# A recurrent attention block and a SiLU block on one core: the state products in quarters of TensorE's columns

## The chip, the core and the metric

The kernel runs on one core of one Trainium2 chip. The metric is the device time of one execution in microseconds, launch to end; the median of repeated runs counts. The kernel before takes 577.69 us (three runs, 577.37 to 578.81).

## What is computed

Two blocks, one behind the other. The first is a gated linear recurrence for 4 batches and 8 heads with 768 tokens and 48 dimensions a head; its output, laid side by side over the heads, feeds a two-layer block with SiLU.

```python
# q, k, v, alpha: (4, 8, 768, 48); alpha between 0.8 and 1.0
for t in range(S):
    state = alpha[:, :, t, :, None] * state + np.einsum('bhd,bhe->bhde', k[:, :, t], v[:, :, t])
    y[:, :, t] = np.einsum('bhd,bhde->bhe', q[:, :, t], state)

x = y.transpose(0, 2, 1, 3).reshape(3072, 384)
h = x @ w_in            # (384, 2048)
g = h * (1.0 / (1.0 + np.exp(-h)))
out = g @ w_out         # (2048, 384)
```

All of it is in fp32.

## The kernel before

The recurrence is cut into chunks of 128 tokens. With 4 batches and 6 chunks in each, 24 chunks are worked through, numbered `n`; `ci` is the place in the sequence, `b` the batch. Two heads make a pair, and a pair lies on 128 partitions: the first head's 48 dimensions on partitions 0 to 47, the second's on 64 to 111, the rest is padding. `NP` is 4 pairs, `D` is 48, `C` is 128.

For a chunk, `products` and `quotient` prepare scaled forms of k and q (`kp`, `qp`); `scores` multiplies them under a causal mask into `g`, and turns `kp` into `kn`, which has the tokens on the partitions; `values` forms y; `states` adds the chunk's contribution to the running state `st`. The state of the last chunk of a batch is not needed, so 20 of the 24 chunks have state products.

`scores`, cut: the products have 48 rows of contraction at partition 0 or 64, and full-width outputs.

```python
        for j in range(NP):
            for u in range(2):
                r = slice(64 * u, 64 * u + D)
                pe.matmul(ps[u][:, j, :], lhsT=c["kp"][r, j, :], rhs=c["qp"][r, j, :],
                          start=True, stop=True)              # L715
        ...
        if ci < NCH - 1:
            ps_k = ps_attn()
            for j in range(NP):
                pe.transpose(ps_k[:, j, :], c["kp"][:, j, :], ident)    # L723
            c["kn"] = work.tile([128, NP, C], F32, name="kn")
            act.copy(c["kn"], ps_k)                           # L725
```

`values` writes y turned, and in quarters: every product has 32 output rows, at partition 0, 32, 64 or 96 of PSUM, so at a quarter of the array's 128 columns. Consecutive products go to different quarters.

```python
        py = ps_attn()
        todo = [(3 * j + i, vn[:, j, at : at + 32], g[:, u, j, :])
                for j in range(NP) for i, at, u in ((0, 0, 0), (1, 32, 0), (2, 80, 1))]
        todo += [(3 * j + 1, vn[:, j, 48:80], g[:, 1, j, :]) for j in range(NP)]
        if ci > 0:
            todo += [(3 * j + i, s[:, j, 32 * i : 32 * i + 32], qp[:, j, :])
                     for j in range(NP) for i in range(3)]
        for i, (at, w, x) in enumerate(todo):
            t, at = divmod(at, 4)
            pe.matmul(py[32 * at : 32 * at + 32, t, :], lhsT=w, rhs=x, ...)   # L749
        ...
        act.copy(xts[half][:, :, e * C : (e + 1) * C], py[:, 0:NKT])          # L754
```

`states` comes next. Its products have 48 output rows, at partition 0 or 64.

```python
            ps = ps_attn()
            for j in range(NP):
                for u in range(2):
                    r = slice(64 * u, 64 * u + D)
                    pe.matmul(ps[r, j, 0:D], lhsT=c["kn"][:, j, r], rhs=vn[:, 2 * j + u, 0:D],
                              start=True, stop=True)          # L764
            for u in range(2):
                r = slice(64 * u, 64 * u + D)
                s, x = st[b][r, :, u, :], ps[r, :, 0:D]
                if ci > 0:
                    dve.tensor_tensor(s, x, s, ALU.add)       # L770
                else:
                    act.copy(s, x)                            # L772
```

`ps_attn()` hands out one of three PSUM buffers in turn; scores, the turned `kp`, y and the states share them.

The two layers of the second block are the large products. They are cut into pieces and put between the stages of the chunks: L807 is the first layer in plain form, L830 the first layer by a scheme with fewer products and more sums, L955 and L928 the second layer in the same two forms. In a step of the main loop the stages stand like this, and `fill` puts pieces behind each slot:

```python
    for step in range(STEPS):
        stages = [[(scores, 1)], [(products, 0)], [(values, 1)], [(states, 1)]]
        if step < GB:                  # GB = 4
            stages = stages[1::-1] + stages[2:]
        elif step >= NA:               # NA = 8
            stages = [[(scores, 1)], [(products, 0)], [(values, 1), (states, 1)], [(quotient, 0)]]
        for slot, group in enumerate(stages):
            for stage, lag in group:
                n = step - lag
                if not 0 <= n < NT:
                    continue
                stage(n)
                ...
            fill(step, slot)
```

The program is not written out strictly in this order: a scheduler places instructions, and may put a later one ahead where an earlier one would have to wait.

The kernel also holds a general path, which runs only when the range of the inputs rules out the quotients; it is not taken here.

Of the kernel before, what the change touches and what calls it, by code (L numbers as in the profile page):

```python
# [355 lines left out]
def quotients(  # L356
# [20 lines left out]
    pe, dve, act, gps = nc.tensor, nc.vector, nc.scalar, nc.gpsimd  # L377
    B, H, S, D = q.shape
# [39 lines left out]
    def ps_attn(n=C):  # L418
        return ps_a.tile([128, 512], F32, name="ps_a").rearrange("p (j c) -> p j c", c=n)
# [335 lines left out]
    def states(n):  # L755
        c = ctxs.pop(n)
        ci, b, vn = c["ci"], c["b"], c["v"]
        if ci < NCH - 1:

            ps = ps_attn()  # L760
            for j in range(NP):
                for u in range(2):
                    r = slice(64 * u, 64 * u + D)
                    pe.matmul(ps[r, j, 0:D], lhsT=c["kn"][:, j, r], rhs=vn[:, 2 * j + u, 0:D],  # L764
                              start=True, stop=True)
            for u in range(2):
                r = slice(64 * u, 64 * u + D)
# [5 lines that stand above are left out]
# [329 lines left out]
    for step in range(STEPS):  # L1102
        stages = [[(scores, 1)], [(products, 0)], [(values, 1)], [(states, 1)]]
        if step < GB:

            stages = stages[1::-1] + stages[2:]
        elif step >= NA:
# [7 lines that stand above are left out]
                if stage is values:  # L1115
                    bridged = n + 1
                if stage is products and n + NIN < NA:
                    load(n + NIN)
                if stage is quotient and n + 1 < NT:
                    load(n + 1)  # L1120
                if stage is states and n + NV < NT:
                    load_v(n + NV)
            fill(step, slot)
            if step >= NA - 1 and slot > 0 and conv_done[1] == NFT and not late:
                settle()
# [20 lines left out]
    ps = ps_attn()[0:1, 0, 0:1]  # L1146
# [64 lines left out]
```

## Time and profile before

| | before |
|---|---|
| median of 3 runs | 577.69 us |
| profiled execution, span | 577.1 us |
| instructions in the profile | 11060 |
| TensorE clock granted | full speed over the whole span |
| DMA | 63.72 MB, 110 GB/s on average |

How to read the profile's views. The page gives each engine's busy time, its share of the span and the number of its instructions; PE is TensorE's matmul, PEld its weight load, which overlaps with matmuls, DVE is VectorE, ACT ScalarE, POOL GpSimd. Below that, the span is cut into 40 equal slices, and each digit is the busy share of a slice in tenths (9 is 90% or more). Matmul ends are modelled, so durations of matmuls that overlap can't be added up; starts and the distances between starts are what to count with.

In the groups of instructions a line has: the line of the kernel, the engine, the operation, output <- inputs, their shapes and types, x count; then busy us and the mean ns of one; then the engine's idle time just before these instructions and what ended it. "issue" is idle time in which the engine waited for nothing that the profile shows. In the view of waits the numbers are the total in us, how many times, and the longest. In the timeline a line has: start in us, duration in us, engine and line, operation, shapes, x how many were merged, and in brackets the idle time before. An fp32 product of this kernel makes two matmul records and two weight loads, a transpose one of each.

### The profile page before, as it was taken

What the parts mean: (1) busy time and instruction counts of PE and PEld (TensorE: products, weight loads), DVE (VectorE), ACT (ScalarE), POOL (GpSimd) and SP (SyncE); (2) the same over time, 40 slices, a digit from 0 to 9 for tenths busy, and PEclk for the clock granted to TensorE, in tenths of its full rate; (3) what the DMA queues carried; (4) which work ended last, traced back from release to release, by engine and by line L of the source; (5) the groups of instructions that cost most, each with busy time, mean ns of one, the idle gap of its engine ahead of it and who ended that gap; (6) DMA issues with size and microseconds to landing.
All of it is one profiled execution on the core that took longest, in us unless ns stands there. A gap on an engine that the chain in (4) does not pass through costs nothing. (4 is left out here: it accounts for less than half of the span.)

```text
span 577.1 us, 11060 instructions
## 1 busy us (share of the span) xinstructions
PE 557.6 (97%) x4450; PEld 491.2 (85%) x4450; DVE 449.3 (78%) x807; ACT 187.6 (33%) x367; POOL 7.3 (1%) x25
## 2 busy tenths in 40 slices
PE   5999999999999999999999999999999999998976
PEld 4677887678998998898998998998998999997976
DVE  5779798999797699995996995996963856747651
ACT  2345543232221233342442442433342331422100
POOL 5000000000000000000000000000000000000000
PEclk9999999999999999999999999999999999999999
DMA  9998784445445414343324333323210123333321
GB/s 212 169 285 215 212 215 118 102 103 139 103 99 129 116 51 120 107 124 84 103 71 118 101 105 85 101 69 89 65 43 9 52 81 115 93 118 98 98 72 30
DMA packets 93900, 63.72 MB, mean 110 GB/s; under 512 B 54800, under 2 KB 85520, under 8 KB 93840
## 3 DMA queue, kind: packets, MB, share of 16 engines
q1 hardware_dynamic: 93840, 62.94, 42.5%
q8 instruction: 36, 0.59, 0.4%
q14 instruction: 24, 0.20, 0.1%
HBM read 58.20 MB, written 4.72 MB: 109 GB/s over the span
## 5 line engine op out<-in xcount | busy, mean ns | idle before, releaser
L928 PE MATMUL ps_o<-w_out,g 128*128 128x192 f32 x704 | 122.8, 328 | 2.3 <-DVE o L942 2.2
L928 PEld LDWEIGHTS ps_o<-w_out,g 128*128 128x128 f32 x704 | 115.2, 190 | 5.6 <-DVE o L942 3.0
L928 PE MATMUL ps_o<-wt,g 128*128 128x192 f32 x528 | 91.6, 326 | 1.3 <-DVE u L1004 1.3
L807 PE MATMUL ps_m<-xt,w_in 128*128 128x256 f32 x384 | 89.6, 384 | 0.8 <-DVE w_in L604 0.5
L928 PEld LDWEIGHTS ps_o<-wt,g 128*128 128x128 f32 x528 | 87.2, 190 | 3.0 <-DVE u L1004 1.6
L807 PEld LDWEIGHTS ps_m<-xt,w_in 128*128 128x128 f32 x384 | 70.7, 190 | 12.2 <-DVE w_in L604 2.9
L830 PE MATMUL ps_m<-xc,w_in 128*128 128x256 f32 x288 | 70.1, 379 | 0.0
L639 DVE TENSOR_REDUCE seen<-bits 128x1 f32<-128x384 int32 (+2 forms) x65 | 42.4, 689 | 30.4 <-DMA bits<-in_moe_w_out_dram 23.9
L830 PEld LDWEIGHTS ps_m<-xc,w_in 128*128 128x128 f32 x288 | 54.0, 190 | 6.4 <-DVE g L844 0.2
L830 PE MATMUL ps_m<-xc,wx 128*128 128x256 f32 x192 | 50.1, 383 | 0.0
L836 ACT COPY g<-ps_m 128x512 f32<-128x512 f32 x64 | 37.0, 586 | 39.8 <-PE ps_m L830 39.8
L933 DVE TENSOR_TENSOR g<-g 128x512 f32<-128x512 f32 x66 | 44.7, 687 | 4.7 <-PE ps_o L928 4.7
L841 ACT ACTIVATE g<-g 128x1024 f32<-128x1024 f32 x32 | 33.2, 1056 | 44.6 <-DVE g L844 44.6
L729 ACT ACTIVATE st<-st,u 128x96 f32<-128x96 f32 x80 | 26.0, 368 | 53.5 <-DVE u L674 38.8
L844 DVE TENSOR_TENSOR g<-ps_m,g 128x512 f32<-128x512 f32 x56 | 37.6, 684 | 2.9 <-PE ps_m L830 2.7
L830 PEld LDWEIGHTS ps_m<-xc,wx 128*128 128x128 f32 x192 | 35.0, 190 | 4.2 <-issue 0.4
L719 DVE TENSOR_TENSOR g<-ps_a,mask 128x512 f32<-128x512 f32 x48 | 31.2, 685 | 6.4 <-PE ps_a L715 6.1
L674 DVE TENSOR_TENSOR_SCAN u<-al,one 128x516 f32<-128x516 f32 x24 | 29.3, 1224 | 6.2 <-ACT al L671 6.1
L699 DVE TENSOR_TENSOR_SCAN p<-al,inv 128x516 f32<-128x516 f32 x24 | 29.5, 1229 | 4.8 <-PE ps_a L749 4.2
L836 ACT COPY part<-ps_m 128x512 f32<-128x512 f32 x32 | 18.8, 587 | 43.6 <-PE ps_m L830 37.8
L810 ACT ACTIVATE g<-ps_m 128x512 f32<-128x512 f32 x32 | 19.0, 594 | 40.6 <-PE ps_m L807 40.5
L715 PEld LDWEIGHTS ps_a<-p,u 48*128 48x128 f32 x384 | 24.8, 193 | 8.1 <-issue 6.5
(117 smaller groups left out, 635.3 us busy)
## 6 DMA issues: line engine op xcount, KB each, us to landing
bits<-in_moe_w_in_dram SPq DMA_DIRECT2D x24, 512.0 KB, 4.2
bits<-in_moe_w_out_dram SPq DMA_DIRECT2D x32, 384.0 KB, 3.4
at<-in_alpha_dram SPq DMA_DIRECT2D x64, 96.0 KB, 2.3
kt<-in_k_dram SPq DMA_DIRECT2D x64, 96.0 KB, 2.4
qt<-in_q_dram SPq DMA_DIRECT2D x64, 96.0 KB, 2.5
vn<-in_v_dram SPq DMA_DIRECT2D x24, 192.0 KB, 3.5
bits<-in_alpha_dram SPq DMA_DIRECT2D x9, 512.0 KB, 3.9
out_dram<-o SPq DMA_DIRECT2D x48, 96.0 KB, 1.8
```

Of the source, the lines that this page charges most:

```text
L639: dve.tensor_reduce(seen[kind][which][:, i : i + 1], x, axis=AX, op=op, apply_absolute_value=True))
L674: dve.tensor_tensor_scan(u[:, end - 1 :: -1], sg[:, end:0:-1], one[:, end:0:-1], 0.0, ALU.mult, ALU.add)
L699: dve.tensor_tensor_scan(p[:, 0:end], sg[:, 0:end], iv[:, 0:end], 0.0, ALU.mult, ALU.add)
L719: dve.tensor_tensor(g[:, u], ps[u], mask[:, None, :].to_broadcast([128, NP, C]), ALU.mult)
L729: act.mul(s[:, j], s[:, j], c["all"][:, j : j + 1])
L807: pe.matmul(ps[:, e, :], lhsT=w_in[:, t, (f + e) * 128 : (f + e + 1) * 128], rhs=xt[:, t, :], start=(t == 0), stop=(t == NKT - 1))
L830: pe.matmul(ps[:, e], lhsT=block_w(w)[:, 2 * pair + e], rhs=block_x(grp, x), start=(first and e == 0), stop=(e == 1), skip_group_check=True)
L836: act.copy(to, ps)
L841: act.activation(x, x, AF.Silu)
L844: dve.tensor_tensor(to, a, b, op)
L928: pe.matmul(ps, lhsT=x, rhs=w[:, i], start=(first and i == 0), stop=(i == HF - 1), skip_group_check=True)
L933: dve.tensor_tensor(cells(grp, h, pair, *to), cells(grp, h, pair, *x), cells(grp, h, pair, *y), ALU.subtract)
```

## The change

The state products are written in quarters of the array's columns: instead of two products of 48 output rows a pair of heads, four of 32. Quarter `i` takes columns 32i to 32i+31 of `kn`, and the v of the head that these belong to. The rows 48 to 63 and 112 to 127 of the PSUM buffer, which come from padding, are written as well now; the instructions that take the result out read the same rows as before. It is for the array to keep the tiling that y, just in front, has used.

```diff
             ps = ps_attn()
             for j in range(NP):
-                for u in range(2):
-                    r = slice(64 * u, 64 * u + D)
-                    pe.matmul(ps[r, j, 0:D], lhsT=c["kn"][:, j, r], rhs=vn[:, 2 * j + u, 0:D],
+                for i in range(4):
+                    r = slice(32 * i, 32 * i + 32)
+                    pe.matmul(ps[r, j, 0:D], lhsT=c["kn"][:, j, r], rhs=vn[:, 2 * j + i // 2, 0:D],
                               start=True, stop=True)
             for u in range(2):
                 r = slice(64 * u, 64 * u + D)
```

## The prediction, made before the changed kernel was run

> **What bounds the kernel now.** I read the head of the page first: busy shares, then the slices over the span.
>
> ```profile
> span 577.1 us, 11060 instructions
> PE 557.6 (97%) x4450; PEld 491.2 (85%) x4450; DVE 449.3 (78%) x807; ACT 187.6 (33%) x367; POOL 7.3 (1%) x25
> ...
> PE   5999999999999999999999999999999999998976
> ...
> DVE  5779798999797699995996995996963856747651
> ```
>
> TensorE is at nine tenths or more from the second slice to the 37th. A busy PE row does not prove that the array streams all the time, so the second view was the waits of PE and of its weight loads between 60 and 470 us: the only wait of the PE row there is one of 0.4 us for VectorE. Only the tail, from 470 us on, has real waits (PE is busy 96.4 of its 107 us), and no state product is left by then: the last starts at 373.4 us. So up to 373 us a nanosecond that PE saves is a nanosecond that everything behind it comes earlier, if nothing takes its place.
>
> The third view, the groups of instructions with shapes kept apart, sizes the line that the change edits (L764) and the one in front of it (L749, y). "x320" counts two records for each fp32 product: 20 chunks of 8 products are 160.
>
> ```profile
> L749 PE MATMUL ps_a<-g,vn 128*32 128x128 f32 x768 | 28.8, 282 | 1.0 <-ACT kn L725 0.7 <-DVE g L719 0.3
> L764 PE MATMUL ps_a<-vn,kn 128*48 128x48 f32 x320 | 11.9, 216 | 0.0
> L764 PEld LDWEIGHTS ps_a<-vn,kn 128*48 128x48 f32 x320 | 9.3, 127 | 4.5 <-issue 4.1 <-DVE w_out L603 0.2 <-ACT st L729 0.2
> ```
>
> All state products together keep PE busy for 11.9 us, 2% of the span. The size of the prize is in the third row: 4.1 us in which the weight load of L764 waited for nothing that the trace can name. The view of all waits of the weight loads tells where such unnamed time sits:
>
> ```profile
> PEld ps_a L749 <- issue: 7.3, 23, 0.5
> PEld ps_a L715 <- issue: 6.5, 22, 0.3
> PEld ps_a L764 <- issue: 4.1, 19, 0.4
> ```
>
> The three longest lines of this view are exactly these three, about once for each run of y (32-wide outputs, all 128 rows), of scores (48 rows) and of states (48-wide outputs). The large products L830 and L928, with six times as many records as L764 (1872 against 320), have at most 0.4 us of it in a group. So it belongs to the change of the array's tiling, not to the products. The fourth view is the timeline of one chunk, weight loads and then products:
>
> ```profile
> 219.39 0.68 PEld L749 LDWEIGHTS ps_a<-p,st 128*32 128x32 f32 x24
> 220.27 0.44 PEld L764 LDWEIGHTS ps_a<-vn,kn 128*48 128x48 f32 x16 [0.20 <-issue]
> 220.76 0.73 PEld L830 LDWEIGHTS ps_m<-xc,wx 128*128 128x128 f32 x4
> ...
> 220.05 0.29 PE L749 MATMUL ps_a<-p,st 128*32 128x128 f32 x4
> ...
> 220.27 0.56 PE L764 MATMUL ps_a<-vn,kn 128*48 128x48 f32 x16
> 220.77 0.48 PE L830 MATMUL ps_m<-xc,wx 128*128 128x256 f32 x1
> ```
>
> **What the Trainium skill says.** "TensorEngine Tiling (Array Packing)", Tiling Modes, Key Properties: changing the tiling mode, not just the tile, drains TensorE. The trace agrees: 0.20 us idle ahead of the first load of states, here and 19 times. The same section: different tiles load and multiply in parallel. The trace agrees for y: 24 loads of 110 ns each take 0.68 us together. "TensorE: Matmul & The Clock Gate", in LDWEIGHTS (loading the stationary operand): the time goes with the columns loaded. In the trace a 32-column load has 110 ns, a 48-column one 125 ns, a 128-column one 190 ns. The same page, Part 1, states a floor of about 25 ns from start to start of small matmuls. States in the trace already start one record per 22 ns on average (below), two tiles side by side, so I take that floor to hold per tile at most.
>
> **The change, part by part.** Each of a chunk's 8 state products, 48 output rows wide at column 0 or 64, becomes two products of 32, at columns 0, 32, 64 and 96, with the same moving data of 48 elements. VectorE and ScalarE read the same rows as before; the added rows 48 to 63 and 112 to 127 are read by nobody. No transfer, no wait of another engine and no buffer changes. Added: 160 products, that is 320 matmul records and 320 loads.
>
> *Cadences now.* In y, the first to last start of 24 loads is 0.68 − 0.11 = 0.57 us; they go in groups of four, so five steps and a few ns: 0.11 us a group, which streams 128 elements. In states it is 0.44 − 0.125 = 0.315 us for eight groups of two: 0.045 us a group, which streams 48.
>
> *What it removes.* The last group of y starts at 220.05. If another group in the same tiling followed, it would start one cadence later, at 220.16. States start at 220.27. The drain costs 0.11 us.
>
> *What it keeps.* Eight groups again (4 pairs of heads, two passes), now of four tiles: if tiles overlap as y's do, 7 x 0.045 = 0.315 us, and about 0.02 us until the fourth tile of the last group has started. The switch from states to full-width products also stays: the last states products start about 0.045 after the last load at 220.585, so 220.63, and L830 comes at 220.77, 0.14 later.
>
> *Sum for a chunk.* Before: 220.05 to 220.77 is 0.72 us. After: 0.11 + 0.315 + 0.02 + 0.14 = 0.585 us. Saved 0.135 us. The first load may gain a little more, because it can now be fetched under y's last group; narrower loads (110 for 125 ns) may shave a few ns off each step. I leave both out.
>
> *How many chunks.* L764 has 272 records after 50 us: 17 chunks. A walk along the PE timeline shows y directly in front of 16 of them, the other (at 78.6 us) stands behind L807, a full-width product, and keeps its drain. Of the first three chunks one ends PE-bound with y in front (26.09 us); in the others PE soon waits for VectorE or a copy anyway (0.30 us at 38.85 us), which eats what they save. So 17 x 0.135 = 2.3 us, all of it on the path: 577.7 − 2.3 = 575.4 us.
>
> **The rivals.**
>
> *1. The array is not fed fast enough.* Twice the instructions in less time: 64 records in about 0.335 us, 5 ns each, where y asks for 112 in about 1.56 us, 14 ns each. If PE's queue cannot be filled like that, states take longer than the drain cost. At a feed of 22 ns a matmul, the mean start distance now, 32 products would take 0.7 us: after becomes 0.11 + 0.7 + 0.14 = 0.95, a loss of 0.23 us a chunk, 581.6 us. Against it: the sequencer's own semaphore records. L723's stands at 294.5 us and L830's at 294.6, with L723's 8 records in between and 0.05 us for the semaphore itself, so roughly 9 ns a record or less; and L723's first load runs only at 295.5, so the queue holds about 1 us of work ahead, which covers much of a burst of 0.3 us. I give it one in ten, mostly in a mild form (0.05 to 0.1 us of the chunk's 0.135 lost again, 576.3 to 577.1 us).
>
> *2. The gain lands in a wait of another engine.* VectorE is busy 84 to 91% between 50 and 350 us. For it: in slices at nine tenths there is little slack, and early on PE does wait for VectorE's weight conversion. Against it: PE has almost no waits from 60 us on, and VectorE gets nothing to do. If half were lost: 576.5 us.
>
> *3. The gap is not the drain but a dependence of states on y's last product.* Both lines share the pool of three PSUM buffers. Then the first load would still wait and only the narrower loads count: 577.5 us. Against it: switches with no such dependence (L928 to scores L715) show a gap of the same kind, 0.23 us on that load.
>
> *4. The order shifts.* Added instructions can make the scheduler place early pieces otherwise; worth perhaps 1 us either way.
>
> **Range and chances.** The centre is 575.4. Full success in all 20 chunks with shorter steps would be about 574.3; rival 2 or 3 in full gives 577.5. Repeats of the kernel before spread over 1.4 us. So 574.2 to 577.2. A gain over 2% would need 11.6 us, nearly all the busy time of the states; a loss over 2% needs rival 1 at over twice its full form.
>
> **What would show each step.** In the changed trace the weight load of L764 should lose its unnamed wait (4.1 us down to under 1), except behind L807; the first states product should start 0.11 us, not 0.22, behind the first of y's last group; loads should come in fours 0.045 us apart; the next line should still start 0.14 us behind the last. L749 and L715 should keep their 7.3 and 6.5 us. The prediction is wrong if groups of four step by clearly more than 0.045 us (rival 1), if the gap stays (rival 3), or if VectorE waits appear ahead of L830 or L928 (rival 2).

## The result and the profile after

| | before | after |
|---|---|---|
| median, first measurement | 577.65 us (577.37 to 578.81, 4 runs) | 575.38 us (574.64 to 576.12, 4 runs) |
| median, measured again later | 579.06 us (19 runs) | 576.37 us (6 runs) |
| ratio, first | | 0.9957 (0.9938 to 0.9976) |
| ratio, second | | 0.9946 (0.9930 to 0.9962) |

The change gains 2.3 and 2.7 us, four to five thousandths. (The ratios come from all runs and are not the quotients of the medians; in brackets stand the intervals of 95%.) The prediction was 575.4 us.

First the head of the page of the changed kernel. 320 matmul records more, 2.8 us of busy PE less:

```profile
span 572.9 us, 11703 instructions
PE 554.8 (97%) x4770; PEld 492.0 (86%) x4770; DVE 449.2 (78%) x807; ACT 187.3 (33%) x367; POOL 7.3 (1%) x25
```

A falling busy time with more products is a warning not to read work off that row: it is the time in which at least one matmul is under way. Next the view of waits of the weight loads (total, times, longest). L764 was third with 4.1 us and is down to 0.8; its two neighbours, whose tilings still change, are as they were:

```profile
PEld ps_a L749 <- issue: 7.5, 24, 0.5
PEld ps_a L715 <- issue: 6.7, 23, 0.3
...
PEld ps_a L764 <- issue: 0.8, 3, 0.3
```

The timeline of the weight loads, in the chunk that the prediction showed, now in the changed kernel:

```profile
218.58 0.68 PEld L749 LDWEIGHTS ps_a<-p,st 128*32 128x32 f32 x24
219.24 0.49 PEld L764 LDWEIGHTS ps_a<-vn,kn 128*32 128x32 f32 x32
219.79 0.73 PEld L830 LDWEIGHTS ps_m<-xc,wx 128*128 128x128 f32 x4
```

The first states load starts 0.66 us after y's last 24 began, ahead of their end; before, it was 0.88 us (219.39 to 220.27), with 0.20 us idle ahead of it. No idle bracket stands on L764 now. From y's last 24 loads to L830 it is 1.21 us, before 1.37. That is 0.16 us for a chunk. The same distance serves for the experiments below.

The matmuls of the same chunk, in the kernel before and in the changed one:

```profile
219.50 0.84 PE L749 MATMUL ps_a<-p,st 128*32 128x128 f32 x24
220.27 0.56 PE L764 MATMUL ps_a<-vn,kn 128*48 128x48 f32 x16
```

```profile
218.68 0.84 PE L749 MATMUL ps_a<-p,st 128*32 128x128 f32 x24
219.34 0.52 PE L764 MATMUL ps_a<-vn,kn 128*32 128x48 f32 x32
```

States start 0.77 us behind the first of these y matmuls before, 0.66 us after: 0.11 us less.

One thing the prediction did not see is in the timeline of PE, near 60 us. The scheduler has put one product of chunk 3 (two records) behind six full-width products, where it costs two changes of tiling for itself:

```profile
59.65 0.52 PE L764 MATMUL ps_a<-vn,kn 128*32 128x48 f32 x30
60.44 2.86 PE L807 MATMUL ps_m<-xt,w_in 128*128 128x256 f32 x12 [0.27 <-ACT xt L754]
63.22 0.27 PE L764 MATMUL ps_a<-vn,kn 128*32 128x48 f32 x2
63.43 2.86 PE L807 MATMUL ps_m<-xt,w_in 128*128 128x256 f32 x12
```

**Where the time went.** The full-width products come in the same order in both programs, so the n-th of one trace can be set against the n-th of the other. Their difference moves in clean steps: 0.155 us at each of 15 chunks, once at chunk 3 a gain of 0.24 and a loss of 0.40, and once, at 238 us, a loss of 0.47 around two waits for VectorE (0.33 and 0.40 us ahead of L830, where before had one of 0.41). By 390 us the changed kernel is 1.6 us ahead in its first profile and 2.0 in its second. The span of its first profile is 4.2 us shorter than that of before, though. The other 2.6 us come behind 490 us, where no state product runs. Either that is an accident of two single profiles, or the change does something there.

### The profile page after: what moved, and what is told of

Its sections match the earlier page's. It is cut to its first block, busy times and chain, and to the rows that moved or that the text cites. A ratio compares the mean times of both kernels' runs of the same rounds, so it can differ in the third digit from the quotient of the medians.

```text
span 572.9 us, 11703 instructions
## 1 busy us (share of the span) xinstructions
PE 554.8 (97%) x4770; PEld 492.0 (86%) x4770; DVE 449.2 (78%) x807; ACT 187.3 (33%) x367; POOL 7.3 (1%) x25
## 5 line engine op out<-in xcount | busy, mean ns | idle before, releaser
L928 PE MATMUL ps_o<-w_out,g 128*128 128x192 f32 x704 | 122.7, 328 | 1.7 <-DVE o L942 1.5
L928 PEld LDWEIGHTS ps_o<-w_out,g 128*128 128x128 f32 x704 | 115.2, 190 | 4.7 <-DVE o L942 2.1
L928 PE MATMUL ps_o<-wt,g 128*128 128x192 f32 x528 | 91.6, 326 | 0.0
L928 PEld LDWEIGHTS ps_o<-wt,g 128*128 128x128 f32 x528 | 87.2, 190 | 1.6 <-DVE u L1004 0.3
L830 PE MATMUL ps_m<-xc,w_in 128*128 128x256 f32 x288 | 70.1, 379 | 0.3 <-DVE g L844 0.3
L830 PEld LDWEIGHTS ps_m<-xc,w_in 128*128 128x128 f32 x288 | 54.0, 190 | 6.8 <-DVE g L844 0.6
L830 PE MATMUL ps_m<-xc,wx 128*128 128x256 f32 x192 | 50.1, 383 | 0.0
L830 PEld LDWEIGHTS ps_m<-xc,wx 128*128 128x128 f32 x192 | 35.0, 190 | 4.2 <-issue 0.4
L715 PEld LDWEIGHTS ps_a<-p,u 48*128 48x128 f32 x384 | 24.5, 193 | 8.1 <-issue 6.7
```

Of the source, the lines that this page charges most:

```text
L830: pe.matmul(ps[:, e], lhsT=block_w(w)[:, 2 * pair + e], rhs=block_x(grp, x), start=(first and e == 0), stop=(e == 1), skip_group_check=True)
L928: pe.matmul(ps, lhsT=x, rhs=w[:, i], start=(first and i == 0), stop=(i == HF - 1), skip_group_check=True)
```

## The experiments

Two theories of the states: **drain** (the gap belongs to the change of tiling and goes when y in front has the same one) against **form** (narrower loads, or more tiles at once, are what is faster). Beside it the question of the feed, and that of the tail.

### The two kernels once more

No edit. The tail from the profiles:

> The kernel before, unchanged, for its profile. Of the 4.2 us that lie between the two profiled spans, 1.6 us had been gained by 390 us, in steps of 0.155 us a chunk; another 2.5 us came in the tail behind 490 us, where no state product runs. Theory A (the tail's waits for the last transfers vary from run to run): time 577.6 us, ratio 1.000 to itself, and this profile's tail (from the last state product to the end) is shorter than the first profile's by 0.5 to 2.5 us. Theory B (the tail gain belongs to the change): the tail is as long as in the first profile, within 0.3 us.

Measured: 579.24 us, ratio 0.9998 (0.9987 to 1.0008), span 577.7 us. Its tail was 0.5 us longer than in the first profile, so neither statement held: it is neither equal within 0.3 us, nor shorter.

> The changed kernel, unchanged, for a tighter interval and a second profile. Drain theory: 17 chunks x 0.135 to 0.155 us less what the early part loses again (about 0.8 us), so 1.6 us from the states; with theory A for the tail the ratio to before is 0.997 (576.0 us), with theory B it is 0.993 to 0.995 (573.5 to 575 us).

Measured: 576.37 us, ratio 0.9946 (0.9930 to 0.9962). That is more than theory A with 1.6 us allowed, and the ratio that theory B named. Its profile says otherwise: behind 490 us this profile gained 0.5 us on the first profile of before, where the first profile of the changed kernel had gained 2.6. The waits of PE behind 490 us account for 2.2 of these 2.6. Kernel before, first profile, then the changed kernel, first and second:

```profile
PE ps_o L928 <- DVE o L942: 2.2, 1, 2.2
PE ps_a L1147 <- DVE good L1143: 1.6, 1, 1.6
PE ps_o L928 <- DVE u L1004: 1.3, 1, 1.3
```

```profile
PE ps_o L928 <- DVE o L942: 1.5, 1, 1.5
PE ps_a L1147 <- DVE good L1143: 1.4, 1, 1.4
```

```profile
PE ps_o L928 <- DVE o L942: 2.4, 2, 2.2
PE ps_a L1147 <- DVE good L1143: 1.4, 1, 1.4
```

In the tail VectorE waits for transfers that feed the range checks (21 to 24 us of waits for those of the second layer's weights alone), and PE for VectorE. The same program shows 2.9 and 3.8 us of this. In the second profile of the changed kernel the granted clock also fell to half from 529.2 to 532.6 us, right behind the wait of 2.2 us: matmuls of L928 started 0.320 us apart there and 0.163 us otherwise, and the stretch took 1.3 us longer than in the first profile. With the 0.9 us of waits that makes the 2.1 us between the two profiles. The kernel before waited as long at this place and kept its clock, so what set it off stays open. A question of a few tenths can't be settled with that in the time.

### Both kernels without the range checks

The checks of alpha and of the weights are left out, with their transfers; the tables that they would fill are set to constants, and the output is computed as before.

```diff
-        for src, n, kind in todo:
+        for kind, value in ((0, 1.0), (1, float(1000 << 20))):
+            for t in seen[kind]:
+                dve.memset(t, value)
+        for src, n, kind in todo[:0]:
```

> The kernel before without the reductions that check the ranges of alpha and of the weights, and without their transfers (37 loads, 65 reductions left out; the tables that they fill are set to constants). It takes the tail's waits for transfers away, which differ from run to run. About 5 us faster than before, 573 us, as PE's waits in the tail (5.1 us in the profile) vanish.

> The changed kernel with the same part left out. Theory A (the states' share of the gain is the sum of the chunks' steps, 1.6 to 2.0 us by 390 us, the rest is the tail's chance alignment with the last transfers): 1.6 to 2.4 us faster than the kernel before with the part left out, and narrow. Theory B (the tail gains from the change by itself): 2.8 us or more faster, or well under 1.5.

Measured: 571.50 us (571.10 to 571.85) and 568.71 us (568.62 to 569.34): 2.79 us, with no overlap and a spread of under a microsecond. By the medians the kernel before is 4.4 us faster for it, where 5 were expected. PE has no wait behind 470 us in either, so its waits there did belong to the checks. Starts of the same full-width product in both timelines:

| behind the states of | before | after | ahead by |
|---|---|---|---|
| chunk 5 | 92.41 | 91.62 | 0.79 |
| chunk 12 | 222.22 | 220.63 | 1.59 |
| chunk 13 | 243.57 | 241.81 | 1.76 |
| chunk 19 | 374.23 | 371.55 | 2.68 |

Behind chunk 19 the lead does not change again up to the last product. So the tail adds nothing of its own: the states' share is 2.7 to 2.8 us here, 14 steps of 0.155 us and 0.6 us from the first four chunks, less 0.1 us around chunk 8, where PE waits for ScalarE and the step is lost. The time alone, 2.79 us, would have spoken for theory B and its 2.8; the starts decide for A in kind, with 2.7 where it had at most 2.4, since the early chunks gave more than it had counted. In the kernels with checks the lead at 390 us was 1.6 to 2.0 us, and the medians say 2.3 and 2.7. The other 0.3 to 1.1 us would have to come from behind 390 us, where the waits of the tail differ from run to run; how much of it would remain over many runs stays open.

### States apart from y

From step 8 on the states are moved one slot later, so that in chunks 7 to 19 full-width pieces stand between y and states; in the kernel before and in the changed one, first with the checks, then without.

```diff
-            stages = [[(scores, 1)], [(products, 0)], [(values, 1), (states, 1)], [(quotient, 0)]]
+            stages = [[(scores, 1)], [(products, 0)], [(values, 1)], [(states, 1), (quotient, 0)]]
```

> The kernel before (48-wide state products) with the states moved one slot later from step 8 on, so that in chunks 7 to 19, 13 of the 20, full-width pieces stand between y and states. Each of these chunks changes tiling twice more to and from full width instead of once from 32 to 48 columns. Drain theory, from the trace of before: one change into full width costs about 0.095 us of drain and about 0.10 us more at its second product (320 instead of 216 ns from start to start); 13 x 0.2 = 2.6 us slower than before, about 1.005. Rival (the gap belongs to states following y, whatever the tiling): no slower, or even 1 us faster.

> The changed kernel with the states moved one slot later in the same way. Drain theory: without y directly in front the quarters save nothing in these 13 chunks; the states run enters behind full-width products with a drain, as the 48-wide run does. Its time is that of the 48-wide kernel with states apart, less only what chunks 3 to 6 gain or lose (0.2 us either way), so within 0.5 us of it and about 2.2 to 3 us slower than the changed kernel as a whole is against before. Rival (narrower weight loads or more tiles side by side make states faster by themselves): 1.5 us or more faster than the 48-wide kernel with states apart.

Measured: 580.45 us, ratio 1.0073 (1.0053 to 1.0093), and 578.70 us, ratio 1.0037 (1.0023 to 1.0052). 1.75 us between them is what the form theory asked for, and the first is 4.6 us above before, where the drain theory had 2.6. But the 11 runs of the second spread from 576.9 to 580.7, and by their traces the two are only 0.12 us apart at 480 us. So both again, without checks; these and the other two kernels without checks below ran on another chip than the first pair (before takes 578.03 us on it, 11 runs; 575.87 us, 16 runs, where the first pair ran). Between the two chips traces are compared rather than times.

> The 48-wide kernel with states one slot later, without the range checks (same part left out as in the pair before), so that the tail no longer blurs the time. Drain theory: each of 13 chunks pays one more change to full width and back; from the trace of the same kernel with the checks, 0.309 us from the last full-width product to states where y to states took 0.202, and two exits. About 2.5 to 4 us slower than the kernel before without checks (571.5 us).

> The quarters with states one slot later, without the range checks. Drain theory: the quarters enter behind full-width products at the same 0.309 us, and gain only 0.017 us a chunk inside the run (0.342 against 0.357 us, and 0.136 against 0.138 behind it); with chunks 5 and 6, where y is still in front, 0.5 us faster than the 48-wide kernel apart, against 2.8 us when together. Rival (the quarters are faster by themselves, as the times with the checks, 578.7 against 580.5 us, could be read): 1.5 us or more.

Measured: 573.52 us (573.32 to 573.85) and 572.54 us (572.39 to 573.23). 0.98 us remain of 2.79. The weight loads of the same chunk, 48-wide and then in quarters:

```profile
224.58 0.44 PEld L767 LDWEIGHTS ps_a<-vn,kn 128*48 128x48 f32 x16 [0.33 <-issue]
225.08 0.46 PEld L931 LDWEIGHTS ps_o<-w_out,g 128*128 128x128 f32 x3
```

```profile
223.76 0.41 PEld L767 LDWEIGHTS ps_a<-vn,kn 128*32 128x32 f32 x32 [0.33 <-issue]
224.23 1.11 PEld L931 LDWEIGHTS ps_o<-w_out,g 128*128 128x128 f32 x7
```

(With the inserted lines, L764 is L767 here, L928 is L931 and so on.) Both have the idle bracket of 0.33 us: behind another tiling the quarters wait as long as the others did. From there to the next line it is 0.50 and 0.47 us. In the paired starts the lead grows by 0.24 us over 13 chunks, 0.018 each; before that, 0.32 us come from chunks 5 and 6, which still have y in front, and 0.4 us from the first chunks. So the form is worth 0.018 of the 0.155 us, the neighbour the rest. The expectation of 0.5 us had left out the first chunks.

The starts of PE tell where the 0.155 us lie. The distances, in us, are those of chunks 5 to 19 behind y (chunk 8 of the quarters left out, where the scheduler mixed some with y) and of 7 to 19 behind full width, and differ by a few ns at most:

| states | from the matmul in front to their first | from their first to their last | from their last to the full-width matmul behind |
|---|---|---|---|
| behind y, 48-wide | 0.202 | 0.357 | 0.138 |
| behind y, quarters | 0.091 | 0.315 | 0.136 |
| behind full width, 48-wide | 0.309 or 0.256 | 0.357 | 0.138 |
| behind full width, quarters | 0.309 or 0.256 | 0.342 | 0.136 |

(It is 0.309 behind matmuls of 256 elements and 0.256 behind those of 192.) The run itself also starts more slowly behind another tiling, by 0.027 us for the quarters. What within a change of tiling takes the time, an emptying of the array or a load that cannot be fetched ahead, no run separates.

The move itself shows the price of a change: between the two 48-wide kernels, together and apart, each chunk loses 0.50 us where the states were, and pays 0.69 where they are now: 0.20 us for one more trip to and from full width, as the drain theory has it. In all, the last product comes 1.7 us later by the traces rather than 2.5 or more, since near 137 us PE waits for ScalarE for 0.5 instead of 1.2 us, and 0.2 us come from before chunk 7.

### Half of the quarters

```diff
-                for i in range(4):
+                for i in (0, 2):
                     r = slice(32 * i, 32 * i + 32)
...
-                r = slice(64 * u, 64 * u + D)
+                r = slice(64 * u, 64 * u + 32)
```

> Only the quarters at columns 0 and 64 of the state products are formed and taken out, so a third of the state's rows is left out; half as many products as in the changed kernel, in the same tiling. Drain theory, with four tiles running side by side: the products left out were free, a chunk's states step 0.042 us a group as before, first to last start about 0.30 against 0.315 us, and the time is that of the changed kernel within 0.3 us. Rival (the feed of instructions limits the group of four): states become shorter by clearly more than 0.02 us a chunk, and 1 us or more is gained in all.

Measured: 576.24 us against 576.37 us of the changed kernel, ratio to before 0.9947 (0.9930 to 0.9964). The loads of the same chunk:

```profile
217.72 0.68 PEld L749 LDWEIGHTS ps_a<-p,st 128*32 128x32 f32 x24
218.38 0.48 PEld L764 LDWEIGHTS ps_a<-vn,kn 128*32 128x32 f32 x16
218.93 0.73 PEld L830 LDWEIGHTS ps_m<-xc,wx 128*128 128x128 f32 x4
```

Again 1.21 us from first to third line, with half as many products, and in the paired starts it gains 0.01 us a chunk on the changed kernel, 0.2 us from chunk 4 to chunk 19. The other two quarters ride along. The feed is not the limit here.

### Every quarter twice

```diff
-                for i in range(4):
+                for i in list(range(4)) * 2:
```

Run without the range checks, to be set against the changed kernel without them.

> The changed kernel without the range checks, with every state product issued twice in a row of four (the second writes the same numbers again): 64 products a chunk instead of 32 records' worth, 128 instructions of PE in one run. Array theory: groups of four step 0.042 us whatever their number, eight groups more are 0.336 us a chunk, 20 chunks 6.7 us: 575.4 us. Rival (the feed of instructions just kept up thanks to the queue): the step grows along the run, to 0.05 us and more, and the time passes 577 us.

Measured: 574.47 us (574.09 to 575.38); by the traces the last product comes 6.3 us later than in the changed kernel without checks. In the same chunk:

```profile
222.97 0.68 PEld L752 LDWEIGHTS ps_a<-p,st 128*32 128x32 f32 x24
223.63 0.83 PEld L767 LDWEIGHTS ps_a<-vn,kn 128*32 128x32 f32 x64
224.52 0.51 PEld L833 LDWEIGHTS ps_m<-xc,wx 128*128 128x128 f32 x3
```

1.55 us, 0.34 more than 1.21: eight groups of four more, 0.0425 us each, the step that the single run has. The paired starts lose 0.34 us at every chunk from chunk 3 on. The 128 instructions of this run (32 products make 64 matmul records and 64 loads) do not slow down, so the rival of the feed falls. The total is a little below 6.7 us: near 136 us a wait gives 0.8 back.

### States right behind y in all chunks from 3 on

```diff
+                    if n >= 3:
+                        tc.keep_in_program_order(mm)     # mm: each state product
...
-        elif step >= NA:
+        elif step < NA:
+            stages = stages[:2] + [[(values, 1), (states, 1)], []]
+        else:
```

> The changed kernel with y and states in one slot from chunk 3 on, and the state products from there pinned in the order they are written. In the changed kernel's trace one product of chunk 3 stands alone between full-width products (it cost 0.40 us there), chunk 4 still has full-width products ahead of its states. Drain theory: chunk 3 gains 0.40 us, chunk 4 loses two changes of tiling and gains 0.3 to 0.45 us; 0.7 to 0.85 us less than the changed kernel, ratio to before 0.001 to 0.0015 lower. Rival (in this early part VectorE's weight conversion sets the pace, and PE's gains turn into its waits): no difference to the changed kernel, and the waits of L807 for VectorE grow by what the states gave.

Measured: 575.70 us, ratio 0.9934 (0.9918 to 0.9950), against 576.37 us and 0.9946 for the changed kernel on the same chip: 0.67 us less, while the intervals against before overlap. In the paired starts against the second profile of the changed kernel chunk 3 gives 0.40 us and chunk 4 0.34, as expected; 0.31 us are lost again at 100 us, with no wait of the kind that the rival named, and the lead is 0.44 us at 390 us. Of the kernels that leave nothing out it has the lowest time on this chip.

### One change of tiling fewer

y and states of a chunk go between the scores of the next and their turned kp. The masked scores get a second buffer for that, and the checks are left out with theirs; large pieces that wait for y are due two slots later.

```diff
+        if n >= NA:                      # in scores(n), ahead of the turning of kp
+            values(n - 1)
+            states(n - 1)
```

> On top of the quarters with states right behind y in all chunks from 3 on, and without the range checks: from chunk 7 on, y and states of one chunk stand between the scores of the next and their turned kp, with a second buffer for the masked scores. A chunk then changes tiling three times (full to 64 rows, to 32 columns, to full) instead of four. Drain theory: one exit to full width and one entry fall away, 0.095 us of drain and 0.10 us at the second full-width product; 16 chunks x 0.2 us = 3.2 us, with 0.5 us of the early chunks: 565 us. Rival 1 (three PSUM buffers: states' buffer waits for the mask of the scores): PE waits for VectorE behind y, little or nothing gained. Rival 2 (y two steps late delays the large products that wait for it): waits or a longer tail.

Measured: 568.46 us (567.98 to 568.90), where 565 was expected; by the traces the last product comes 1.1 us earlier than in the changed kernel without checks, not 3.7. The waits of PE in its profile name rival 1:

```profile
PE ps_a L771 <- DVE g L723: 1.5, 2, 1.3
...
PE ps_a L730 <- DVE g L723: 1.4, 3, 0.5
```

L771 is the states, L730 the turned kp, L723 the mask on the scores: VectorE has not emptied the PSUM buffer that they take. These are 2.9 us in five chunks, about as much as is missing from the 3.7. So an order that saves changes of tiling has to leave VectorE its time.

## Why the prediction was right, and where its sum was not

- **What bounds the kernel** held: up to 374 us nearly each step of a chunk reached the next full-width product whole, and the run without checks kept all of it to the end.
- **The drain, 0.11 us**, held in size and place: the first state matmul follows y's last by 0.202 us before and 0.091 us after, while behind full width both follow alike. The exit to full width stayed, as predicted (0.138 and 0.136 us).
- **Eight groups at 0.045 us** was a little too long: the step is 0.0425 us. Over seven steps that makes the 0.02 us by which 0.155 us a chunk exceeds the predicted 0.135. The prediction had named narrower loads and left them out; the quarters apart from y measured them as 0.018.
- **17 chunks, 2.3 us** was right in total, partly by luck, and wrong in its parts. 15 chunks gave a full step, 2.3 us. Chunk 3 lost 0.16 because of one stray product (rival 4), 0.47 us were lost around VectorE waits near 238 us (rival 2, once; not in the kernels without checks), and the first chunks, of which only one had been counted, gave up to 0.8 us, or lost 0.1, depending on what they then waited for. The lead before the tail was 1.6 to 2.0 us; that the first median shows just 2.3 took something from the tail.
- **The feed** (rival 1) was wrong by the runs with half and double the quarters; **a dependence on y's last product** (rival 3) by the gap's vanishing.
- **The floor of about 25 ns** from start to start, which the Trainium skill states ("TensorE: Matmul & The Clock Gate", Part 1), is at most one for each tile: 64 matmuls in four tiles started 0.0425 / 4 = 0.0106 us apart on average. Here the measurement decides.
- **Waits of L749 and L715 unchanged** held (7.5 and 6.7 us against 7.3 and 6.5).
- **Small slips**: the nines of the PE row end with the 36th slice, not the 37th, and the 32 products of rival 1's sum are matmul records.
- **What was not predicted**: the tail. Its waits moved a single profile by 2 us, nearly as much as the whole effect.

## What to carry to other kernels

Look at unnamed idle time ahead of weight loads: where it stands at changes of tiling, matching the tiling of neighbours removes it, and it is worth more products to do so as long as their tiles run side by side. The change back to full width hardly shows in that view (0.4 us in all ahead of L830), though it costs time too; distances between starts show both. Small runs pay most: here a trip out of full width and back costs 0.20 us, over half of a states run of 0.36. To measure such tenths, take the waits that differ from run to run out of both kernels, and set the starts of unchanged instructions against each other; a span alone misled here by 2 us.

## What the runs showed of the hardware

PE takes instructions faster than I had estimated from the trace of before: 64 loads and 64 matmuls, 128 instructions, passed in about 0.68 us (16 groups of 0.0425 us), 5 ns each, where I had estimated 9 ns or less; some of them may have stood in its queue beforehand. And a change of tiling into full width has a second part behind the drain: the second full-width matmul (256 elements) starts 320 instead of 216 ns after the first, about 0.10 us, in before and after alike.
